# Who copies a transposed pair, and what VectorE does first: slots 5 to 8 of a fused attention and two-layer kernel

## The chip, the core and the metric

The kernel runs on one core of a Trainium2 chip. The core has five engines with a queue each, which they work off in order: TensorE (PE: matmuls, transposes), VectorE (DVE), ScalarE (ACT), GpSimd (POOL) and SyncE (SP); DMAs run beside them. Matmuls write to PSUM, a memory of eight banks from which VectorE and ScalarE read. Engines wait for each other through semaphores. The metric is the device time of one execution in microseconds, median of three runs.

## The reference

For each of 8 batches and 8 heads (sequence S = 576, head width 64) an attention with a decay that comes from a forget gate `f`, and then, over all 4608 tokens, two matrix products with an elementwise function between them:

```
scores = q @ k.T / 8 + (cum[:, None] - cum[None, :])   # cum = cumsum(log(clip(f)))
attn   = softmax(scores with the causal mask);  x = attn @ v
h = x @ w_in            # 512 -> 2048
g = h - tanh(h)
out = g @ w_out         # 2048 -> 512
```

## The kernel before

The attention goes pair by pair of heads: 32 pairs, four to a batch, and the loop at L608 has one slot `p` for each pair, and one more. Slot p holds the scores of pair p in seven tiles (`TILES`, numbers 0 to 6; tile 3 is small and holds the last block of both heads), and pieces of other work put between the tiles by `att_items(p)`. The order is written out by hand: what is emitted first stands first in the queue of its engine.

- `scores` (L306): one to four matmuls of KT and QT into a PSUM bank `ps` (pool `ps_sc`, two banks), then ScalarE's exp into `e` (L335), then from batch 1 on a mask by GpSimd (L345). So the scores of tile t need the bank that the exp of tile t-2 has read.
- `values` (L350): 30 matmuls of `e` and v into `av` for the pair before, and on VectorE the division by the row sums: an add (L364), a reciprocal (L365) and a product into `xn` (L366).
- `turn` (L369): turns `xn` into XR, the input of the products, from slot 5 on by two transposing DMAs on SP's queue.
- `trans` (L254): six transposes on TensorE turn one pair of q or k (rows 6n to 6n+5 of a head lie on one partition) into one PSUM bank, `t32`; from slot 4 on the bank comes from `ps_tr`, which has one. Then it is copied into QT or KT. With `split` false there are two copies, each of both heads: one of the even tokens (partitions 0 to 63 of the bank), one of the odd (64 to 127). With `split` true there are four, one for each head and half, in the order head 0 even, head 0 odd, head 1 even, head 1 odd. The letters in `copies` say which engine makes each: V for VectorE (L277), A for ScalarE (L275). `trans` emits the first two copies and returns the rest, which only the start of the program (L519 on) uses.
- `mlp1(u, ft)` (L398): four matmuls of win and XR into `hps` (pool `ps_m`, three banks), the tanh `th` on ScalarE (L413; pool `tmp`, two buffers), and VectorE's sum of both into `gq` (L417). u counts groups of 512 tokens, ft blocks of 128 columns.
- `mlp2_plain` (L436) for u = 0, `mlp2` (L455) after that: the second product. For u > 0 it goes by a scheme of seven products instead of eight, with sums and differences on VectorE (`sums`) and of the weights (`weights`, L243).

In slots 0 to 3 (`early`) the transposes use other banks. Slots 4 to 6 each transpose q and k of the next pair, by VectorE alone (`"VV"`); in slots 5 and 6 q's stands after tile 0 (`at_q`), k's after tile 3 (`at_k`), and `values` of the pair before after tile 2. The 16 column blocks of `mlp1` for u = 0 are spread over slots 4 to 6: blocks 4 to 10 in slot 5, and blocks 11 to 15 and the first step of `mlp2_plain` in slot 6. Slots 7 and 8 have four transposes each, after tiles 0, 2, 4 and 6 (L569 to L571): q and k of two pairs of batch 2, with `"VA"`. These two slots also have steps of `mlp2_plain` and VectorE's differences of the weights. From batch 3 on q and k are turned by DMA.

Of the kernel before, what the change touches and what calls it, by code (L numbers as in the profile page):

```python
# [11 lines left out]
ALU = mybir.AluOpType  # L12
# [9 lines left out]
def kernel(  # L22
# [10 lines left out]
    nc = tc.nc  # L33
    P = 128

    B, H, S, D = q.shape
# [4 lines left out]
    NPAIR = H // 2  # L41
    NJ = 5
# [38 lines left out]
    qn, kn = ([t[0:S // NT6, :].rearrange("p (h n d) -> p h n d", h=H, n=NT6) for t in raw] for raw in (qraw, kraw))  # L81
    qb, kb = ([t[:, 0:NJ * DM].rearrange("p (n e) -> p n e", n=NJ) for t in raw] for raw in (qraw, kraw))
    vn = [qkp.tile([P, NJ, H, VW], FP16, tag=f"vn{i}", name=f"vn{i}") for i in range(2)]
    QT = [qkp.tile([D + 3, H, S], FP16, tag=f"QT{i}", name=f"QT{i}") for i in range(2)]
    KT = [qkp.tile([D + 3, H, PITCH], FP16, tag=f"KT{i}", name=f"KT{i}") for i in range(2)]
# [89 lines left out]
    def const_rows(i):  # L175
        nc.sync.dma_start(out=QT[i][D:D + 2, :, :], in_=minus16)
        nc.sync.dma_start(out=KT[i][D + 2:D + 3, :, 0:S], in_=ones16[0:H, :])
# [74 lines left out]
    E, XN, GQ, SQ, M2 = {}, {}, {}, {}, {}  # L252

    def trans(b, c, src, dst, early, copies, split=False):  # L254
        pn, g3 = S // NT6, NT6 // 2
        if early:
            t32 = ps_m.tile([P, UW], FP32, tag="m", name="t32")
            t16 = t32.bitcast(FP16)[:, 0:2 * S // 2].rearrange("p (a g n) -> p a g n", a=2, g=g3)
        else:
            t32 = ps_tr.tile([P, UW], FP32, tag="tr", name="t32")  # L260
            t16 = t32.bitcast(FP16)[:, 0:2 * S // 2].rearrange("p (a g n) -> p a g n", a=2, g=g3)
        for a in range(2):
            for g in range(g3):
                nc.tensor.transpose(out=t16[:, a, g, :],  # L264
                                    in_=src[b % 2][:, 2 * c + a, 2 * g:2 * g + 2, :],
                                    identity=id16[0:pn, 0:pn])
        parts = [(a, e) for a in range(2) for e in range(2)] if split else [(slice(0, 2), e) for e in range(2)]

        def copy(a, e, eng):
            if split:  # L270
                a = slice(a, a + 1)
            to = dst[b % 2][0:D, 2 * c:2 * c + 2, e:S:2].rearrange("d a (p g) -> d a p g", g=g3)[:, a]
            of = t16[e * D:(e + 1) * D, :, :, :].rearrange("d a g p -> d a p g")[:, a]
            if eng == "A":
                nc.scalar.activation(out=to, in_=of, func=AF.Copy)  # L275
            else:
                nc.vector.tensor_copy(out=to, in_=of)  # L277

        todo = [lambda a=a, e=e, eng=eng: copy(a, e, eng) for (a, e), eng in zip(parts, copies)]
        for fn in todo[:2]:  # L280
            fn()
        return todo[2:]

    def head_tiles(a):
        return [[(a, 0, 0, 512, 0)],
# [61 lines left out]

    AV = {}

    def values(b, c, heads=(0, 1)):  # L350
        if 0 in heads:
            AV[(b, c)] = ps_av.tile([P, 2, 512], FP32, tag="av", name="av")
        av = AV[(b, c)][:, :, 0:NJ * (D + 1)].rearrange("p a (i d) -> p a i d", i=NJ)
        for a in heads:
            for ib in range(NJ):
                for j in range(ib + 1):
                    nc.tensor.matmul(out=av[:, a, ib, :], lhsT=E.pop((b, c, a, j, ib)),  # L357
                                     rhs=vn[b % 2][:, j, 2 * c + a, 0:D + 1],
                                     start=(j == 0), stop=(j == ib))
        if 1 not in heads:  # L360
            return
        xn = XN[(b, c)] = fin.tile([P, NJ, P], FP16, tag="xn", name="xn")
        rs = fin.tile([P, 2, NJ, 1], FP32, tag="rs", name="rs")
        nc.vector.tensor_scalar_add(out=rs, in0=av[:, :, :, D:D + 1], scalar1=1e-9)  # L364
        nc.vector.reciprocal(out=rs, in_=rs)  # L365
        nc.vector.tensor_tensor(out=xn.rearrange("p i (a d) -> p a i d", a=2), in0=av[:, :, :, 0:D],  # L366
                                in1=rs.to_broadcast([P, 2, NJ, D]), op=ALU.mult)

    def turn(b, c):  # L369
        xn = XN.pop((b, c))  # L370
# [18 lines left out]
    def bank(name):  # L389
        ring = RINGS[turn_of[0]]  # L390
        pool = ring[turn_of[1] % len(ring)]
        turn_of[1] += 1
        return pool.tile([P, UW], FP32, tag=TAGS[pool], name=name)
# [4 lines left out]
    def mlp1(u, ft, part=None):  # L398
        if part != 1:
            HP[(u, ft)] = bank("hps")  # L400
        hps = HP[(u, ft)]
        t0 = u * UW % RING
        parts = [(0, t0, min(UW, RING - t0))]
        if t0 + UW > RING:
            parts.append((RING - t0, 0, t0 + UW - RING))
        for o, t, n in parts:
            for ci in {None: range(NCH), 0: range(NCH - 1), 1: (NCH - 1,)}[part]:
                nc.tensor.matmul(out=hps[:, o:o + n], lhsT=win[:, ci, ft * P:(ft + 1) * P],  # L408
                                 rhs=XR[:, ci, t:t + n], start=(ci == 0), stop=(ci == NCH - 1))
        if part == 0:  # L410
            return
        th = tmp.tile([P, UW], FP32, tag="th", name="th")
        nc.scalar.activation(out=th, in_=hps, func=AF.Tanh, scale=-1.0)  # L413
        half, i, kt = ft // NK, ft % NK // 4, ft % 4
        if half == 0 and kt == 0:
            GQ[(u, i)] = gtp.tile([P, 2, NK // 2, UW], FP16, tag="gq", name="gq")
        nc.vector.tensor_tensor(out=GQ[(u, i)][:, half, kt, :], in0=hps, in1=th, op=ALU.add)  # L417
        if u >= PLAIN:
            if ft in (3, 6, 9, 12):
                sums(u, "S3", ft // 3 - 1)  # L420
# [8 lines left out]
    def sums(u, name, n):  # L429
        i, ks = n // 2, slice(n % 2 * 2, n % 2 * 2 + 2)  # L430
        if name == "S2" and n % 2 == 0:
            SQ[(u, i)] = gtp.tile([P, 2, NK // 2, HU], FP16, tag="sq", name="sq")
        x, y, op = SUMS[name]
        nc.vector.tensor_tensor(out=LHS[name](u, i)[:, ks], in0=LHS[x](u, i)[:, ks], in1=LHS[y](u, i)[:, ks], op=op)
# [112 lines left out]
    def att_items(p):  # L547
        def put(fn, *args):
            items.append((lambda: fn(*args), True))

        items = []
        here = pairs[p] if p < len(pairs) else None
        before = pairs[p - 1] if 0 < p <= len(pairs) else None
        after = pairs[p + 1] if p + 1 < len(pairs) else None
        early = p < NPAIR
        for ti in range(len(TILES)):
            if here and (p > 0 or ti > 1):
                put(scores, *here, ti)
            if p == 1 and ti == 6:
                items.append((lambda: const_rows(1), False))  # L560
                items.append((lambda: load_aug(1), False))
            if early and p > 0 and ti in (0, 6):
                put(unread, 2)
            if p == 1 and ti == 3:
                put(last)
            for load in LOADS.get((p, ti), ()):
                items.append((load, False))
            at_q, at_k = (1, 3) if p == 0 else (0, 1) if early else (0, 2) if p == NPAIR else (0, 3)
            if p in (2 * NPAIR - 1, 2 * NPAIR) and ti % 2 == 0:  # L569
                pair = pairs[2 * NPAIR + 2 * (p - 2 * NPAIR + 1) + ti // 4]  # L570
                put(trans, *pair, *((kn, KT) if ti % 4 else (qn, QT)), False, "VA")  # L571
            if ti == at_q and p < 2 * NPAIR - 1:
                put(trans, *after, qn, QT, early, "VV")
            if p == NPAIR:
                if ti in (3, 4):
                    put(mlp1, 0, ti - 3, 1)
            if ti == at_k and p < 2 * NPAIR - 1:
                put(trans, *after, kn, KT, early, "VV")
            if p == NPAIR:
                if ti == 1:  # L580
                    put(turn, *pairs[p - 2])
                    put(values, *before)
                    put(mlp1, 0, 0, 0)
                elif ti == 2:
                    put(mlp1, 0, 1, 0)
                    put(turn, *before)
            elif early and ti in (2, 3) and before:
                put(values, *before, (ti - 2,))
            elif not early and ti == 2 and before:
                put(values, *before)  # L590
            if p < NPAIR:
                if ti == 1 and p > 1:
                    put(turn, *pairs[p - 2])
            elif p > NPAIR and ti == 3:
                put(turn, *before)
        return items

# [8 lines left out]
    with tc.manual_schedule(engines=FIVE):  # L606
        bulk()
        for p in range(len(pairs) + 1):  # L608
            b, c = divmod(p, NPAIR)
            items = att_items(p)  # L610
# [50 lines left out]
```

## Time and profile before

| what | value |
|---|---|
| median of three runs | 347.95 us (347.94 to 347.99) |
| profiled execution: its time, its span | 347.95 us, 346.2 us |
| busy: PE, PEld, DVE, ACT, POOL | 335.2, 230.6, 261.7, 232.6, 161.3 us |
| chain that ended last, by engine | PE 87%, DVE 6%, ACT 4% |
| granted TensorE clock | 1.00 |

The span goes from the first to the last instruction of the trace; the rest of the time lies around it. Busy time of PE is that of matmuls whose ends are modelled, so that they overlap: a matmul of 512 columns is shown with 0.38 us and the next of its kind starts 0.22 us after it. A row of the timeline gives start, duration, engine, line, operation, and in brackets the idle time before it with what ended it. `L277 DVE COPY KT<-t 64x576 f16` is a copy by VectorE, of 64 partitions and 576 elements on each.

### The profile page before, as it was taken

Reading aid. Unit: us, or ns where it says so; the run is one execution under the profiler, and the core shown is the slowest. Engines: PE = TensorE matmul, PEld = TensorE weight load, DVE = VectorE, ACT = ScalarE, POOL = GpSimd, SP = SyncE. Lnnn points to the kernel's source line nnn. Section 1 sums busy time; section 2 is a strip of 40 time slices with the busy share of each in tenths; the row PEclk is TensorE's granted clock in tenths of the full one; section 3 lists DMA queues with packets and bytes.
Section 4 is the critical chain, followed back from the end, with each engine's and each line's share of the span. In section 5 each row is a group of like instructions: output and inputs, shape, how many; then the busy total and the mean of one; then the engine's idle time right before and its main releaser. Section 6 shows DMA issues by size and latency. Waiting matters only on the chain.

```text
span 346.2 us, 8606 instructions
## 1 busy us (share of the span) xinstructions
PE 335.2 (97%) x3253; PEld 230.6 (67%) x3253; DVE 261.7 (76%) x504; ACT 232.6 (67%) x437; POOL 161.3 (47%) x319
## 2 busy tenths in 40 slices
PE   8988998889999999999999999999999999999995
PEld 7476554555578656865688888755875587487485
DVE  6599787564988788678867886788677766876874
ACT  5687886777897787778767876788548842632640
POOL 8974652676558655765577465742322210000000
PEclk9999999999999999999999999999999999999999
DMA  8999999999999999799979997991131013003003
GB/s 108 147 182 201 193 201 154 107 114 177 132 130 105 177 137 122 94 176 137 117 78 200 130 128 78 186 143 27 49 97 31 17 50 110 0 14 109 0 11 113
DMA packets 144877, 38.80 MB, mean 112 GB/s; under 512 B 128148, under 2 KB 143236, under 8 KB 144836
## 3 DMA queue, kind: packets, MB, share of 16 engines
q0 software_dynamic: 92480, 18.39, 69.7%
q1 hardware_dynamic: 52356, 19.88, 30.5%
q8 instruction: 25, 0.41, 0.5%
q14 instruction: 16, 0.13, 0.1%
HBM read 36.85 MB, written 9.44 MB: 134 GB/s over the span
## 4 chain that ended last, share of the span: by engine, by line
PE 87%; DVE 6%; ACT 4%; issue 1%; DMA 1%; ACTq 0%
PE hps L408 32%; PE ops L466 28%; PE ps L326 12%; PE av L357 8%; PE ops L442 3%; DVE gq L417 2%; ACT e L335 2%; DVE QT L277 2%; PE t L264 1%; DVE KT L277 1%; PE ps L329 1%; DMA TQ<-in_f_dram 1%; PE ps L297 1%; ACT QT L275 1%; ACT th L413 1%
## 5 line engine op out<-in xcount | busy, mean ns | idle before, releaser
L408 PE MATMUL hps<-XR,win 128*128 128x512 f16 (+1 forms) x640 | 140.9, 357 | 0.9 <-ACT XR L378 0.7
L413 ACT ACTIVATE th<-hps 128x512 f32<-128x512 f32 x144 | 86.9, 603 | 55.4 <-PE hps L408 54.6
L335 ACT ACTIVATE e<-ps 128x512 f16<-128x512 f32 x192 | 110.5, 598 | 14.1 <-PE ps L326 6.0
L417 DVE TENSOR_TENSOR gq<-hps,th 128x512 f16<-128x512 f32 x144 | 98.4, 688 | 26.0 <-ACT th L413 24.6
L345 POOL TENSOR_SCALAR_AFFINE_SELECT e<-e 128x128 f16<-128x128 f16 x168 | 60.4, 361 | 78.0 <-ACT e L335 76.1
L408 PEld LDWEIGHTS <-win 128*128 128x128 f16 x640 | 57.7, 97 | 48.4 <-issue 0.5
L326 PE MATMUL ps<-QT,KT 67*128 67x64 f16 (+5 forms) x384 | 77.9, 276 | 3.1 <-ACT e L335 1.7
L466 PEld LDWEIGHTS <-gq 128*128 128x128 f16 x640 | 60.4, 97 | 11.1
L466 PE MATMUL ops<-wout,gq 128*128 128x256 f16 x512 | 63.2, 272 | 0.0
L326 PEld LDWEIGHTS <-KT 67*128 67x128 f16 (+1 forms) x384 | 36.7, 98 | 25.5 <-DVE KT L277 1.6
L357 PEld LDWEIGHTS <-e 128*128 128x128 f16 x896 | 32.2, 97 | 3.9
L357 PE MATMUL av<-vn,e 128*128 128x65 f16 x896 | 33.6, 193 | 0.0
L119 POOL DMA_DIRECT2D vn<-in_v_dram x32 | 28.0, 878 | 8.7 <-DMA win<-in_moe_w_in_dram 4.1
L466 PE MATMUL ops<-W,sq 128*128 128x256 f16 x256 | 31.2, 272 | 0.0
L366 DVE TENSOR_TENSOR xn<-av,rs 128x640 f16<-128x640 f32 x32 | 26.4, 825 | 1.1
L466 PEld LDWEIGHTS <-sq 128*128 128x128 f16 x256 | 24.2, 98 | 3.4
L96 POOL DMA_DIRECT2D kn<-in_k_dram x25 | 21.2, 848 | 1.5 <-issue 1.3
L345 POOL TENSOR_SCALAR_AFFINE_SELECT el<-el 128x128 f16<-128x128 f16 x28 | 9.4, 334 | 26.9 <-ACT el L335 26.2
L96 POOL DMA_DIRECT2D qn<-in_q_dram x25 | 21.2, 848 | 1.3 <-issue 0.8
L364 DVE TENSOR_SCALAR rs<-av 128x10 f32<-128x10 f32 x32 | 5.2, 162 | 19.0 <-PE av L357 17.9
L277 DVE COPY QT<-t 64x576 f16<-64x576 f16 x18 | 14.5, 803 | 6.2 <-PE t L264 6.1
L277 DVE COPY KT<-t 64x576 f16<-64x576 f16 (+1 forms) x22 | 16.3, 739 | 3.8 <-PE t L264 3.6
(82 smaller groups left out, 307.5 us busy)
## 6 DMA issues: line engine op xcount, KB each, us to landing
out_dram<-ost SPq DMA_DIRECT2D x34, 256.0 KB
vn<-in_v_dram POOLq DMA_DIRECT2D x24, 128.0 KB, 5.6
qn<-in_q_dram POOLq DMA_DIRECT2D x20, 128.0 KB, 4.3
kn<-in_k_dram POOLq DMA_DIRECT2D x20, 128.0 KB, 4.6
win<-in_moe_w_in_dram POOLq DMA_DIRECT2D x2, 1024.0 KB, 14.8
wout<-in_moe_w_out_dram POOLq DMA_DIRECT2D x2, 1024.0 KB, 14.1
XR<-xn SPq DMA_TRANSPOSE x56
vn<-in_v_dram POOLq DMA_DIRECT2D x12, 64.0 KB, 5.2
```

The source lines that it names most:

```text
L96: nc.gpsimd.dma_start(out=dst[b % 2][0:pn, n, :].rearrange("p (h d) -> p h d", h=H), in_=src[b, :, n * P:n * P + pn, :].rearrange("h p d - ...
L119: nc.gpsimd.dma_start(out=vn[b % 2][:, n, h0:h1, 0:D], in_=v[b, h0:h1, n * P:(n + 1) * P, :].rearrange("h p d -> p h d"))
L277: nc.vector.tensor_copy(out=to, in_=of)
L326: nc.tensor.matmul(out=ps[:, col:col + n], lhsT=KT[b % 2][0:rows, h, j * P:(j + 1) * P], rhs=QT[b % 2][0:rows, h, i0:i0 + n], start=not ow ...
L335: nc.scalar.activation(out=e[:, lo:hi], in_=ps[:, lo:hi], func=AF.Exp, scale=qscale)
L345: nc.gpsimd.affine_select(out=view, in_=view, compare_op=ALU.is_ge, fill=0.0, base=0, pattern=pat, channel_multiplier=-1)
L357: nc.tensor.matmul(out=av[:, a, ib, :], lhsT=E.pop((b, c, a, j, ib)), rhs=vn[b % 2][:, j, 2 * c + a, 0:D + 1], start=(j == 0), stop=(j == ib))
L366: nc.vector.tensor_tensor(out=xn.rearrange("p i (a d) -> p a i d", a=2), in0=av[:, :, :, 0:D], in1=rs.to_broadcast([P, 2, NJ, D]), op=ALU. ...
L408: nc.tensor.matmul(out=hps[:, o:o + n], lhsT=win[:, ci, ft * P:(ft + 1) * P], rhs=XR[:, ci, t:t + n], start=(ci == 0), stop=(ci == NCH - 1))
L413: nc.scalar.activation(out=th, in_=hps, func=AF.Tanh, scale=-1.0)
L417: nc.vector.tensor_tensor(out=GQ[(u, i)][:, half, kt, :], in0=hps, in1=th, op=ALU.add)
L466: nc.tensor.matmul(out=ps[:, m, :], lhsT=LHS[lhs](u, kt // 4)[:, kt % 4, m * P:(m + 1) * P], rhs=rhs[:, kt, :], start=(fresh and (apart or ...
```

## The change

It has two parts. In slots 7 and 8 the transposes are copied with `"VVAA"` and `split` true, and `trans` emits all four copies at once: VectorE copies head 0 (even and odd tokens), ScalarE head 1. There `values`, which stood behind the transposes of k after tile 2, is put ahead of them.

In slots 5 and 6 `values` no longer emits the division but leaves it in a list, `HELD`. While that list is not empty, the sums of `mlp1` (L417) are appended to it too. After tile 3, behind the transposes and copies of k and ahead of `turn`, the list is emitted in its order.

```
-        for fn in todo[:2]:
+        now = 4 if copies == "VVAA" else 2
+        for fn in todo[:now]:
             fn()
-        return todo[2:]
+        return todo[now:]
...
+    HELD = []
+
+    def release():
+        while HELD:
+            HELD.pop(0)()
+
-    def values(b, c, heads=(0, 1)):
+    def values(b, c, heads=(0, 1), hold=False):
...
-        nc.vector.tensor_scalar_add(out=rs, in0=av[:, :, :, D:D + 1], scalar1=1e-9)
-        nc.vector.reciprocal(out=rs, in_=rs)
-        nc.vector.tensor_tensor(out=xn.rearrange("p i (a d) -> p a i d", a=2), in0=av[:, :, :, 0:D],
-                                in1=rs.to_broadcast([P, 2, NJ, D]), op=ALU.mult)
+
+        def divide():
+            nc.vector.tensor_scalar_add(out=rs, in0=av[:, :, :, D:D + 1], scalar1=1e-9)
+            nc.vector.reciprocal(out=rs, in_=rs)
+            nc.vector.tensor_tensor(out=xn.rearrange("p i (a d) -> p a i d", a=2), in0=av[:, :, :, 0:D],
+                                    in1=rs.to_broadcast([P, 2, NJ, D]), op=ALU.mult)
+
+        HELD.append(divide)
+        if not hold:
+            release()
...
-        nc.vector.tensor_tensor(out=GQ[(u, i)][:, half, kt, :], in0=hps, in1=th, op=ALU.add)
+
+        def add_up():
+            nc.vector.tensor_tensor(out=GQ[(u, i)][:, half, kt, :], in0=hps, in1=th, op=ALU.add)
+
+        if HELD:
+            HELD.append(add_up)
+        else:
+            add_up()
...
             if p in (2 * NPAIR - 1, 2 * NPAIR) and ti % 2 == 0:
+                if ti == 2:
+                    put(values, *before)
                 pair = pairs[2 * NPAIR + 2 * (p - 2 * NPAIR + 1) + ti // 4]
-                put(trans, *pair, *((kn, KT) if ti % 4 else (qn, QT)), False, "VA")
+                put(trans, *pair, *((kn, KT) if ti % 4 else (qn, QT)), False, "VVAA", True)
...
-            elif not early and ti == 2 and before:
+            elif p in (NPAIR + 1, NPAIR + 2) and ti == 2:
+                put(values, *before, (0, 1), True)
+            elif not early and ti == 2 and before and p not in (2 * NPAIR - 1, 2 * NPAIR):
                 put(values, *before)
...
             elif p > NPAIR and ti == 3:
+                items.append((release, False))
                 put(turn, *before)
```

## The prediction

> **What bounds the kernel now.** I read the busy time by stretches first, to see where TensorE is not full. Columns: busy us and (instructions) of each engine, granted clock, DMA share, GB/s.
>
> ```profile
> 43.00:56.50 13.50, 12.16 (x104) 6.41 (x102) 12.36 (x21) 10.11 (x20) 6.35 (x16) 1.00 1.52 193
> 56.50:80.00 23.50, 21.03 (x196) 11.87 (x197) 12.99 (x22) 16.73 (x28) 13.71 (x27) 1.00 1.42 126
> 80.00:120.00 40.00, 40.00 (x394) 26.77 (x393) 32.53 (x63) 31.52 (x61) 27.17 (x50) 1.00 1.42 140
> ```
>
> From 80 us on TensorE is busy without a gap (also in the stretches to 280 and 320), at a granted clock of 1.00. A delay or a gain that exists at 80 us therefore reaches the end one for one: no later idle time takes a delay in. Slots 5 to 8, which the change touches, lie in the first two stretches (slot 5 about 38 to 47 us, slot 6 to 56.6, slot 7 to 66.6, slot 8 to 77.1). Next, TensorE's waits:
>
> ```profile
> PE ps L326 <- ACT e L335: 1.7, 5, 0.5
> PE t L264 <- ACT QT L275: 1.7, 4, 0.4
> PE ps L326 <- DVE KT L277: 1.1, 1, 1.1
> PE t L264 <- ACT KT L275: 0.3, 1, 0.3
> PE hps L408 <- DVE gq L417: 0.2, 1, 0.2
> ```
>
> The wait on KT is the first score of slot 7. The waits of `t` are transposes that need their only PSUM bank (`ps_tr`, one buffer) back. Then the timeline of VectorE, ScalarE and TensorE around them (start, us, engine, line):
>
> ```profile
> 43.80 0.82 DVE L366 TENSOR_TENSOR xn<-av,rs 128x640 f16<-128x640 f32 x1
> 44.54 0.68 DVE L417 TENSOR_TENSOR gq<-hps,th 128x512 f16<-128x512 f32 x1
> 45.14 1.60 DVE L277 COPY KT<-t 64x576 f16<-64x576 f16 x2
> 46.77 2.11 DVE L417 TENSOR_TENSOR gq<-hps,th 128x512 f16<-128x512 f32 x3
> ```
> ```profile
> 45.32 0.60 ACT L413 ACTIVATE th<-hps 128x512 f32<-128x512 f32 x1 [0.31 <-PE hps L408]
> 47.56 0.60 ACT L413 ACTIVATE th<-hps 128x512 f32<-128x512 f32 x1 [0.67 <-DVE gq L417]
> ```
> ```profile
> 45.51 1.03 PE L408 MATMUL hps<-XR,win 128*128 128x512 f16 x4
> 47.52 1.02 PE L408 MATMUL hps<-XR,win 128*128 128x512 f16 x4 [0.20 <-DVE gq L417]
> 56.57 0.39 PE L326 MATMUL ps<-QT,KT 67*128 67x512 f16 x1 [1.10 <-DVE KT L277]
> 59.82 0.41 PE L264 MATMUL t<-id,kn 96*128 96x96 f16 x6 [0.43 <-ACT QT L275]
> ```
> ```profile
> 58.12 0.80 DVE L277 COPY QT<-t 64x576 f16<-64x576 f16 x1 [0.88 <-PE t L264]
> ```
> ```profile
> 58.95 0.81 ACT L275 ACTIVATE QT<-t 64x576 f16<-64x576 f16 x1 [1.29 <-DVE QT L277]
> ```
>
> Two things matter. At 47.52 and 47.56 both TensorE and ScalarE wait for one `gq` sum: `hps` has three banks and `th` two buffers, so the sum of column block n frees the bank of block n+3 and the buffer of block n+2. And the transpose at 57.66 ends at 58.08, VectorE copies 58.12 to 58.92, and only then, 0.03 us later, ScalarE copies to 59.77: the two copies of one transpose run one after the other, in all eight transposes of slots 7 and 8, 0.80 + 0.03 + 0.81 = 1.65 us. Last, the prices by form:
>
> ```profile
> L277 DVE COPY QT<-t 64x576 f16<-64x576 f16 x18 | 14.5, 803 | 6.2 <-PE t L264 6.1
> L275 ACT ACTIVATE QT<-t 64x576 f16<-64x576 f16 x4 | 3.2, 812 | 3.3 <-DVE QT L277 3.3
> L275 ACT ACTIVATE QT<-t 64x288 f16<-64x288 f16 x4 | 2.0, 489 | 1.2 <-PE t L264 1.1
> L277 DVE COPY KT<-t 64x288 f16<-64x288 f16 x4 | 1.9, 476 | 0.1
> ```
>
> **Slot 5: the held sum.** In the order of the changed program VectorE does: sums 5 and 6, k's two copies, the division (L364 to L366), sum 7, sums 8 and on. Only sum 7 is held back. The kn transposes end at 43.51, so the copies run 43.55 to 45.16 (1.60), the division to 46.46 (43.36 to 44.63 before, 1.27 with its gaps), sum 7 to 47.05 (44.54 + 0.68 = 45.22 before), sum 8 to 47.66. Sum 7 is 1.83 later. Queued behind it: TensorE's block 10 needs its bank and goes from 45.51 to 47.11; ScalarE's tanh of block 9 needs its buffer and goes from 45.32 to 47.15. Behind that tanh stand the exps of tiles 4 and 5 on ScalarE (cadence 0.48): they end 48.23 and 48.72. TensorE's tile 6 waits for the bank of tile 4 (48.28, was 46.45) and slot 6's first score for that of tile 5 (48.77, was 46.94); block 11 starts 0.22 later at 48.99 instead of 47.52. Loss 1.47. The 0.20 wait for sum 8 and the 0.11 wait before slot 6's first score go, both hidden inside this.
>
> **Slot 6: what the order gains.** From 48.99 TensorE repeats its cadence (7.57 us from block 11 to tile 6): tile 6 at 56.56. K's copies now run 54.56 to 56.17, ahead of the division, so the first score of slot 7 (KT) no longer waits for them; late next is the bank of tile 5, whose exp ends at 57.00 (block 15's tanh at 55.42, then exps at 0.48). It starts at 57.05: 0.49 us after tile 6, against 55.09 to 56.57, 1.48, before. Gain 0.99. Sum 14 is held too, but no tanh follows it before slot 9, and `ops` in slot 7 needs it only at 60.6, when it has been done since 58.1. The division ends 3.1 us later (57.5 against 54.4), and with it the two transposing DMAs to XR on SP; the first matmul that reads XR for block u=1 is past 82 us, and SP has nothing to issue between 57 and 62 but these.
>
> **Slots 7 and 8: the split copies.** Each transpose now has four 64x288 copies: VectorE two for head 0, 2 x 0.476 + 0.01 = 0.97; ScalarE two for head 1, 2 x 0.49 + 0.01 = 1.00. In the built program ScalarE's first copy still waits for the count that VectorE's second copy brings, so a transpose takes 0.97 + 0.03 + 1.00 = 2.00 us where it took 1.65: 0.35 more, eight times. If the wait were not there it would take about 1.0; this is the lower end of the unknown cost, and the first rival. I take 2.00, because the eight rows of before show the wait and the changed program keeps it.
> The row first: ScalarE's eight copies start 0.03 us behind VectorE's, never beside them. The Trainium skill, "PSUM — Partial Sum Buffer", section "PSUM bank collisions raise a hardware error", says that two engines must not touch one bank in the same 32-partition quadrant at once, reads with reads included, and calls guarding by bank the simple version; both heads of a transpose lie in the same partitions of one bank. By that rule the copies stay in turn, and the sum is the one here; its finer form, by quadrant, would have let the old halves (partitions 0 to 63 and 64 to 127) run together, and the trace does not show that.
>
> Now the path, with the latencies of before (TensorE's end to a copy 0.04, a copy's end to TensorE 0.05, to the next exp 0.02). k's transposes of tile 2 also stand behind `values` and one `ops` step now, at no cost in TensorE's work, but VectorE's division stands ahead of their copies. Transposes a to d are slot 7's, e to h slot 8's. Starting from 57.05:
> a at 58.13 (57.66 before), copies done 60.63; b at 61.46 (59.82), no wait, its old 0.59 wait is covered by values and ops (1.77 us). av starts 59.69, the division runs 60.80 to 62.07, b's copies to 62.96 and 64.00, so c, wanted at 63.73, starts 64.05 (63.85). c's copies end 66.52: d, wanted 65.64, starts 66.57 (66.00). The exp of tile 5 stands behind c's copies on ScalarE and ends 67.14: slot 8's first score 67.19 (66.62). d's copies end 69.03: e, wanted 68.27, starts 69.08 (68.14). f at 72.41 (70.29 with its 0.59 wait, which values and ops cover). Division to 73.0, f's copies to 74.94: g at 74.98 (74.32). g's copies, behind slot 8's last `ost`, end 77.44: h at 77.49 (76.47). Slot 9's first score waits for the exp of tile 5: 78.11 (77.09). h's copies end 79.95 on ScalarE and hold back slot 9's first exp to 80.57, which frees the bank of tile 2: 80.62 (79.25).
> From slot 7's first score to there: 23.57 against 22.68, loss 0.89. The waits that the move removes (two of 0.59) are less than what the longer copies add at c, d, e, g, h and behind.
>
> **Sum.** +1.47 − 0.99 + 0.89 = +1.37 us at 80 us, carried to the end. The profiled execution took 347.95 (span 346.2 and 1.7 outside it), which is the median of the runs too: 349.3. ScalarE's extra (8 x 0.19) and VectorE's (8 x 0.17) are inside this; the weights' differences (L245) move behind copies, but are read from slot 10 on.
>
> **The rivals.**
> Side by side: if the copies of the two heads did overlap, each transpose would be free 1.0 us after its end. Redoing the same path, the waits at b, c, d, f and g go, h and e keep 0.2 and 0.4, slot 9's first score is at 75.26: 1.83 earlier than before, 346.1. It decides as soon as ScalarE's copy starts over 0.5 us before VectorE's second ends. Against it: the eight rows and the kept wait. A page speaks for it: the Trainium skill, "Perfetto Trace Analysis", section "Optimizing Scalar/DVE Operations", says that breaking up instructions may let work finish sooner where an engine makes others idle; here no reader of the bank is served by half of it.
> The held sum costs nothing: if block 10's bank or the tanh's buffer came from elsewhere, slot 5 stays as it is, and −0.99 + 0.89 leaves −0.1: 347.85, no change. It decides if sum 7 ended before 45.5. Against it: 47.52 and 47.56 show exactly this dependence for the next sum.
> No recovery in slot 6: if VectorE's lag pushed k's copies past 57 again, as in the 1.10 wait of before, the 0.99 is lost: 350.3. Against it: they end 0.9 before they are needed.
>
> **How the numbers follow.** 0.2% is 0.7 us, about what a measurement of this kernel tells from no change. Forecast 0.71 (its own range 348.7 to 349.9, a third of a microsecond of error in each of the three parts), no recovery 0.08, held sum free 0.08, side by side 0.13. The range 347.6 to 350.4 takes in all but the last. Slower takes the forecast, but for a few parts in a hundred near the bound, and no recovery: 0.77; same 0.11; faster 0.12.
>
> **What would show it.** In the new trace: one wait of TensorE's `hps` on VectorE's sum of about 1.5 us near 47 us; no wait on KT at slot 7; ScalarE's 64x288 copies 0.03 us behind VectorE's second; `t` waiting near 66, 69 and 77 us by 0.8 to 0.9; the stretch after 82 us as before, only later. Wrong if ScalarE's copies begin together with VectorE's, or if the first score of slot 6 stands before 48 us.

## The result, and the profile after

The changed kernel takes 349.69 us (median of six runs, 349.67 to 351.36) against 347.95 (347.93 to 347.99): a ratio of 1.0058, 95% interval 1.004 to 1.0076 (of the means; the medians alone give 1.0050). It is 1.74 us slower; forecast were 1.35 more, 349.3. Single executions of several of these kernels take 1.5 to 3 us longer than the others (351.36 here), which leaves the median where it is but raises the mean.

Its line numbers differ from those of before: L421 is `hps` (was L408), L426 the tanh (L413), L432 the sum (L417), L375 the division's product (L366), L336 the exp (L335), L327 the scores (L326), L462 `ops` of u = 0 (L442). L264, L275 and L277 are as they were. First the busy time by stretches, cut at 57.05, where slot 7 begins, and at 82.00, in slot 9 behind the last wait that the slots cause (columns: busy us and instructions of PE, PEld, DVE, ACT, POOL; granted clock; DMA share; GB/s):

```profile
43.00:57.05 14.05, 12.25 (x104) 6.58 (x103) 11.71 (x20) 9.42 (x20) 5.79 (x14) 1.00 1.51 192
57.05:82.00 24.95, 21.61 (x198) 12.03 (x198) 14.90 (x31) 18.53 (x37) 16.32 (x28) 1.00 1.21 122
82.00:120.00 38.00, 38.00 (x385) 25.95 (x384) 31.18 (x61) 29.95 (x58) 25.52 (x48) 1.00 1.42 130
```

TensorE is again full from 82 us on, at a clock of 1.00. Set instruction against instruction, TensorE is 1.48 us later in slot 6, 1.65 at the first `hps` of slot 9, and still 1.65 at 225 us: what the slots lose reaches the end. (0.07 more comes near 230 us. It shows in the trace of the part in slots 7 and 8 alone too, not in that of slots 5 and 6; its cause is open.) TensorE's waits:

```profile
PE ps L327 <- ACT e L336: 2.1, 7, 0.5
PE t L264 <- ACT QT L275: 1.6, 2, 0.8
PE hps L421 <- DVE gq L432: 1.4, 1, 1.4
PE t L264 <- ACT KT L275: 1.1, 3, 0.7
```

The wait of a score for KT (1.1 before) is gone. In its place stand one wait of `hps` for a sum, 1.4 us (0.2 before), and waits of `t` that are as many but longer: 2.7 us over five times against 2.0 over five. The timelines of slot 5 (VectorE; ScalarE; TensorE, with the first score of slot 7 last):

```profile
43.55 1.61 DVE L277 COPY KT<-t 64x576 f16<-64x576 f16 x2
45.63 0.82 DVE L375 TENSOR_TENSOR xn<-av,rs 128x640 f16<-128x640 f32 x1
46.38 2.10 DVE L432 TENSOR_TENSOR gq<-hps,th 128x512 f16<-128x512 f32 x3
```
```profile
47.15 0.60 ACT L426 ACTIVATE th<-hps 128x512 f32<-128x512 f32 x1 [2.14 <-DVE gq L432]
```
```profile
47.11 1.02 PE L421 MATMUL hps<-XR,win 128*128 128x512 f16 x4 [1.43 <-DVE gq L432]
48.99 1.03 PE L421 MATMUL hps<-XR,win 128*128 128x512 f16 x4
57.06 0.38 PE L327 MATMUL ps<-QT,KT 67*128 67x512 f16 x1
```

Copies, division, then the sums: the first of the three sums from 46.38 on is that of block 7, which the list had held, and both TensorE's block 10 and ScalarE's tanh of block 9 start right behind it. And slot 7's and 8's copies (VectorE; ScalarE; TensorE's transposes):

```profile
64.55 0.97 DVE L277 COPY QT<-t 64x288 f16<-64x288 f16 x2 [1.01 <-PE t L264]
```
```profile
65.61 0.98 ACT L275 ACTIVATE QT<-t 64x288 f16<-64x288 f16 x2 [0.78 <-DVE QT L277]
```
```profile
64.09 0.41 PE L264 MATMUL t<-id,qn 96*128 96x96 f16 x6 [0.20 <-ACT KT L275]
66.65 0.42 PE L264 MATMUL t<-id,kn 96*128 96x96 f16 x6 [0.79 <-ACT QT L275]
69.20 0.41 PE L264 MATMUL t<-id,qn 96*128 96x96 f16 x6 [0.69 <-ACT KT L275]
```

VectorE's two copies of the transpose at 64.09 end at 65.52, ScalarE's start at 65.61 and end at 66.60, and the next transpose starts at 66.65. The two engines copy in turn, as before, only longer: 0.97 + 0.09 + 0.98 = 2.04 us against 1.65.

### The profile page after: what moved, and what is told of

The parts are those of the page before. It is cut to its first block, busy times and chain, and to the rows that moved or that the text cites. A ratio compares the mean times of both kernels' runs of the same rounds, so it can differ in the third digit from the quotient of the medians.

```text
span 348.0 us, 8637 instructions
## 1 busy us (share of the span) xinstructions
PE 335.4 (96%) x3253; PEld 230.5 (66%) x3253; DVE 263.0 (76%) x512; ACT 233.5 (67%) x445; POOL 163.0 (47%) x319
## 4 chain that ended last, share of the span: by engine, by line
PE 91%; DVE 3%; ACT 3%; issue 1%; DMA 1%; ACTq 0%
PE hps L421 35%; PE ops L486 28%; PE ps L327 13%; PE av L364 8%; PE ops L462 2%; PE t L264 2%; ACT e L336 1%; DVE KT L277 1%; PE ps L330 1%; DMA TQ<-in_f_dram 1%; PE ps L298 1%; ACT KT L275 1%; PE ps L296 0%; DVE TQ L159 0%; PE x L390 0%
## 5 line engine op out<-in xcount | busy, mean ns | idle before, releaser
L421 PE MATMUL hps<-XR,win 128*128 128x512 f16 (+1 forms) x640 | 140.9, 357 | 2.1 <-DVE gq L432 1.4
L426 ACT ACTIVATE th<-hps 128x512 f32<-128x512 f32 x144 | 86.9, 603 | 56.9 <-PE hps L421 54.8
L432 DVE TENSOR_TENSOR gq<-hps,th 128x512 f16<-128x512 f32 x144 | 98.4, 688 | 26.8 <-ACT th L426 25.3
L336 ACT ACTIVATE e<-ps 128x512 f16<-128x512 f32 x192 | 110.4, 598 | 12.2 <-PE ps L330 4.8
L346 POOL TENSOR_SCALAR_AFFINE_SELECT e<-e 128x128 f16<-128x128 f16 x168 | 62.1, 371 | 78.5 <-ACT e L336 76.6
L421 PEld LDWEIGHTS <-win 128*128 128x128 f16 x640 | 57.8, 97 | 49.8 <-issue 1.8
L327 PE MATMUL ps<-QT,KT 67*128 67x64 f16 (+5 forms) x384 | 77.9, 276 | 2.5 <-ACT e L336 2.1
L327 PEld LDWEIGHTS <-KT 67*128 67x128 f16 (+1 forms) x384 | 36.8, 98 | 24.6 <-issue 2.1
L375 DVE TENSOR_TENSOR xn<-av,rs 128x640 f16<-128x640 f32 x32 | 26.4, 825 | 1.1
L277 DVE COPY QT<-t 64x576 f16<-64x576 f16 (+1 forms) x22 | 15.1, 685 | 6.9 <-PE t L264 6.7
L277 DVE COPY KT<-t 64x576 f16<-64x576 f16 (+1 forms) x26 | 16.9, 650 | 3.2 <-PE t L264 2.8
```

Of the source, the lines that this page charges most:

```text
L327: nc.tensor.matmul(out=ps[:, col:col + n], lhsT=KT[b % 2][0:rows, h, j * P:(j + 1) * P], rhs=QT[b % 2][0:rows, h, i0:i0 + n], start=not ow ...
L336: nc.scalar.activation(out=e[:, lo:hi], in_=ps[:, lo:hi], func=AF.Exp, scale=qscale)
L346: nc.gpsimd.affine_select(out=view, in_=view, compare_op=ALU.is_ge, fill=0.0, base=0, pattern=pat, channel_multiplier=-1)
```

## The experiments

The theory: the change is two parts that add. In slots 5 and 6 the held sum costs and the early copies gain; in slots 7 and 8 the split copies cost, because both heads lie in one PSUM bank, and the earlier `values` gains. The rivals: the held sum is harmless; the division ahead of k's copies is what costs; the copies are kept in turn by their destination and not by the bank. Times of before in these runs: 347.95 and 347.97. The diffs are against the changed kernel where they say "changed", else against the kernel before.

**The part in slots 5 and 6 alone** (changed kernel, slots 7 and 8 put back)

```
-                if ti == 2:
-                    put(values, *before)
...
-                put(trans, *pair, *((kn, KT) if ti % 4 else (qn, QT)), False, "VVAA", True)
+                put(trans, *pair, *((kn, KT) if ti % 4 else (qn, QT)), False, "VA")
...
-            elif not early and ti == 2 and before and p not in (2 * NPAIR - 1, 2 * NPAIR):
+            elif not early and ti == 2 and before:
```

> The part in slots 5 and 6 alone (division and late sums behind k's copies); slots 7 and 8 as before. If the parts add up as in the prediction: slot 5 loses 1.47 (block 10 and the tanh of block 9 wait for the held sum 7), slot 6 gains 0.99, so slot 7's first score stands at 57.05 instead of 56.57 and all after it is 0.48 later: 348.4 us. Rival, the held sum costs nothing: block 10 stays near 45.5 and the time is 347.0. Rival, slot 6 gives nothing back: 349.4.

Measured: 348.48 us, ratio 1.0029 (1.0016 to 1.0042). TensorE in slot 5 and at slot 7's first scores:

```profile
47.09 1.02 PE L421 MATMUL hps<-XR,win 128*128 128x512 f16 x4 [1.43 <-DVE gq L432]
56.54 0.87 PE L327 MATMUL ps<-QT,KT 67*128 67x320 f16 x3
57.25 1.03 PE L462 MATMUL ops<-wout,gq 128*128 128x512 f16 x4
```

Block 10 waits as in the full change, and the first score of slot 7 follows the last of slot 6 in one row: the wait on KT is gone. The `ops` behind it stood at 56.80 before. Loss and recovery are both there, 0.53 net; both rivals on this part fall.

**The part in slots 7 and 8 alone** (changed kernel, nothing held)

```
-            elif p in (NPAIR + 1, NPAIR + 2) and ti == 2:
-                put(values, *before, (0, 1), True)
```

> The part in slots 7 and 8 alone (split copies, values ahead of k's transposes); slots 5 and 6 as before. By the prediction's path this part costs 0.89; with the gap of 0.09 instead of 0.03 us between VectorE's second copy and ScalarE's first, which the changed kernel's trace shows, 1.17: 349.1 us. Rival, the parts depend on each other (VectorE's lag from slot 6 makes slot 7 slow): nearer to before, under 348.6.

Measured: 349.24 us, ratio 1.0056 (1.0034 to 1.0079): +1.29. With +0.53 of the other part that makes +1.82, and the whole change is +1.74: the parts add, but for 0.08.

**Only the division held, the sums where they were** (the first experiment, and:)

```
-        if HELD:
-            HELD.append(add_up)
-        else:
-            add_up()
+        add_up()
```

> As the part in slots 5 and 6 alone, but only the division is held back, the sums are emitted where they were. Sum 7 then ends near 44.5, so block 10 and the tanh of block 9 do not wait; but sum 8 stands behind copies and division and ends near 48.0 instead of 47.47, so block 11 is some 0.5 late; slot 7's first score near 56.2 instead of 56.57: 347.6 us. If the held sum is not what makes slot 5 slow, the time is that of the part with the sums held, 348.4.

Measured: 347.32 us, ratio 0.9982 (0.9973 to 0.999). ScalarE's tanh of block 9 and TensorE's first score of slot 7:

```profile
45.28 0.60 ACT L426 ACTIVATE th<-hps 128x512 f32<-128x512 f32 x1 [0.27 <-PE hps L421]
```
```profile
55.74 0.39 PE L327 MATMUL ps<-QT,KT 67*128 67x512 f16 x1 [0.26 <-DVE KT L277]
```

The tanh waits for its own matmuls again, and the part gains 0.63 instead of losing 0.53. The difference, 1.16 us, is what holding the sums costs: those of blocks 7 and 8 in slot 5 and that of block 14 in slot 6. It gained 0.3 more than expected: sum 8 came ahead of the division too, since block 8 is emitted before the list is (so the changed kernel holds its sum as well), and block 11 did not wait; in its place block 12 waited 0.24 for sum 9.

**Only `values` moved in slots 7 and 8, copies as before**

```
             if p in (2 * NPAIR - 1, 2 * NPAIR) and ti % 2 == 0:
+                if ti == 2:
+                    put(values, *before)
...
-            elif not early and ti == 2 and before:
+            elif not early and ti == 2 and before and p not in (2 * NPAIR - 1, 2 * NPAIR):
```

> Only values put ahead of k's transposes in slots 7 and 8; copies unsplit as before (VectorE even tokens, ScalarE odd), slots 5 and 6 as before. If the longer copies are what costs in slots 7 and 8, the move itself is a gain: values and one ops step cover the bank's release at the second and the sixth transpose, two waits of 0.59 go and none comes: 346.8 us. Rival, the division ahead of k's copies is what costs: the third and the seventh transpose wait, and the time is 348 or more.

Measured: 346.81 us, ratio 0.9967 (0.9955 to 0.9979). Transposes a to d of slot 7:

```profile
57.66 0.42 PE L264 MATMUL t<-id,qn 96*128 96x96 f16 x6
60.99 0.42 PE L264 MATMUL t<-id,kn 96*128 96x96 f16 x6
63.26 0.42 PE L264 MATMUL t<-id,qn 96*128 96x96 f16 x6
65.41 0.41 PE L264 MATMUL t<-id,kn 96*128 96x96 f16 x6 [0.42 <-ACT QT L275]
```

The second waits no more, and the third doesn't wait although the division now stands ahead of k's copies. The move is a gain of 1.14, twice the wait of 0.59; the rival that blames the division falls.

**Only the copies split, `values` where it was** (and `trans` emits all four copies, as in the change)

```
-                put(trans, *pair, *((kn, KT) if ti % 4 else (qn, QT)), False, "VA")
+                put(trans, *pair, *((kn, KT) if ti % 4 else (qn, QT)), False, "VVAA", True)
```

> Only the split copies (VectorE head 0, ScalarE head 1, one bank) in slots 7 and 8; values where they were, slots 5 and 6 as before. If the copies stay in turn, a transpose's bank is free 2.06 us after its end instead of 1.65: the four waits of 0.59 and the one of 0.44 grow by 0.4 to 0.46 each, and slot 9's third tile waits 0.4: +2.4 to +2.7, 350.4 to 350.7 us. If the split itself were harmless and the division ahead of the copies the cost: 348 or less.

Measured: 350.47 us, ratio 1.0067 (1.0052 to 1.0082): +2.50. Transposes b, d and e:

```profile
60.23 0.42 PE L264 MATMUL t<-id,kn 96*128 96x96 f16 x6 [0.83 <-ACT QT L275]
66.82 0.42 PE L264 MATMUL t<-id,kn 96*128 96x96 f16 x6 [0.83 <-ACT QT L275]
69.37 0.41 PE L264 MATMUL t<-id,qn 96*128 96x96 f16 x6 [0.69 <-ACT KT L275]
```

Each wait of 0.43 (as the profile counts it, from the modelled end) has become 0.83. The split alone is the loss, and the move takes 1.23 of it back (350.47 to 349.24).

**The two heads in two banks** (the part in slots 7 and 8 alone, and the edit below; transposes and copies of head a then use `t16[a]`)

```
+        elif copies == "VVAA":
+            t16 = [pool.tile([P, UW], FP32, tag=tag, name="t32").bitcast(FP16)[:, 0:S // 2]
+                   .rearrange("p (a g n) -> p a g n", a=1, g=g3) for pool, tag in ((ps_tr, "tr"), (ps_m, "m"))]
         else:
```

> As the part in slots 7 and 8 alone (349.24), but head 1 of each transpose goes to a bank of its own (from the three of ps_m), so VectorE and ScalarE read different banks. If the shared bank is what keeps the copies in turn, ScalarE's first copy starts 0.04 us after the transposes end, beside VectorE's; a bank is free after 1.05 us and the waits of the transposes go: by the path 345.5 us. If it is the destination (one QT or KT tile for both) or something else, ScalarE still starts behind VectorE and the time stays near 349.2 or above.

Measured: 345.28 us, ratio 0.9926 (0.9905 to 0.9946). VectorE's and ScalarE's copies of the first transpose of slot 7 (L283 and L281 here), and their mean by form (four of ScalarE's twelve belong to the start of the program):

```profile
57.99 0.97 DVE L283 COPY QT<-t 64x288 f16<-64x288 f16 x2 [0.76 <-PE t L267]
```
```profile
58.12 0.99 ACT L281 ACTIVATE QT<-t 64x288 f16<-64x288 f16 x2 [0.46 <-PE t L267]
```
```profile
L281 ACT ACTIVATE QT<-t 64x288 f16<-64x288 f16 x12 | 5.9, 488 | 2.0 <-PE t L267 1.9
L283 DVE COPY QT<-t 64x288 f16<-64x288 f16 x8 | 3.8, 478 | 2.5 <-PE t L267 2.5
```

ScalarE's copies start when head 1's transposes end (58.08), beside VectorE's, in spite of the common destination QT, and none of the single copies is slower for it (478 and 488 ns; 476 and 489 before). In all eight transposes ScalarE starts before VectorE's second copy ends, by 0.08 to 1.05 us. The part in slots 7 and 8 goes from a loss of 1.29 to a gain of 2.69. Both hold the 1.14 that the move gains by itself; without it, the split costs 2.43 in one bank and gains 1.55 in two. The common bank was the reason that the copies went in turn; as a bank is also one tile of the program here, the run does not tell the bank from the tile. Head 1's bank comes from a pool of three, and so seldom has to be waited for; an estimate from the ends of ScalarE's copies in this trace is that one second bank alone would have held up two of the eight transposes, by 0.15 and 0.03 us. The rule cited in the prediction (the Trainium skill, "PSUM — Partial Sum Buffer", "PSUM bank collisions raise a hardware error") agrees with this, and so does a sentence of that page's section "Specifications (TRN2)", that the two engines read PSUM in parallel at full rate as long as they don't meet in a bank. No run shows what the chip would do without the wait: it is set when the program is built, and was not taken away.

**The two gaining halves together** (changed kernel, only slot 6 held, copies unsplit)

```
-            elif p in (NPAIR + 1, NPAIR + 2) and ti == 2:
+            elif p == NPAIR + 2 and ti == 2:
...
-                put(trans, *pair, *((kn, KT) if ti % 4 else (qn, QT)), False, "VVAA", True)
+                put(trans, *pair, *((kn, KT) if ti % 4 else (qn, QT)), False, "VA")
```

> The gaining halves together: division and late sum held in slot 6 alone (slot 5 as before), values ahead of k's transposes in slots 7 and 8, copies unsplit. If slot 6's gain of 0.99 and the move's 1.14 (measured alone) add up: 345.8 us. If slot 6's gain was only the recovery of time lost in slot 5, it is that of the move alone, 346.8.

Measured: 345.78 us, ratio 0.9932 (0.9915 to 0.9948): −2.19; less the 1.14 of the move, slot 6 gives 1.05. Slot 6's gain is its own, and not a recovery of what slot 5 lost.

**A version without these waits** (changed kernel, only slot 6 held; the transposes after tiles 4 and 6 copied by VectorE alone, the one after tile 6 in a bank of `ps_m`)

```
-            t32 = ps_tr.tile([P, UW], FP32, tag="tr", name="t32")
+            t32 = (ps_m if other else ps_tr).tile([P, UW], FP32, tag="m" if other else "tr", name="t32")
...
-                put(trans, *pair, *((kn, KT) if ti % 4 else (qn, QT)), False, "VVAA", True)
+                put(trans, *pair, *((kn, KT) if ti % 4 else (qn, QT)), False, "VV" if ti > 3 else "VA", False, ti == 6)
```

> A version that takes the waits away: division and late sum held in slot 6 alone, values moved, and the transposes after tiles 4 and 6 copied by VectorE alone, the one after tile 6 in a bank of ps_m. ScalarE's exp of tile 5 then stands behind no copy, and no transpose needs a bank in use. All waits of slots 6 to 8 (4.8 us) but about 0.3 would go: 343.5 us if VectorE, with 5 us more to do in slots 7 and 8, keeps up; up to 345 if it becomes late with the division or slot 9's sums.

Measured: 343.62 us, ratio 0.9879 (0.9858 to 0.99): the fastest of all, 4.35 below before. Its busy time in slots 7 and 8 (columns as above; all rows of this trace stand 1.9 us later from the first slots on, so the cut is later):

```profile
58.50:80.00 21.50, 21.50 (x232) 12.92 (x230) 17.08 (x29) 13.91 (x26) 17.14 (x31) 1.00 1.54 134
```

TensorE is busy without a gap there, and VectorE, with 17.08 of 21.50 us, keeps up.

## Why the prediction came out as it did

**Where delays go.** That everything at 80 us is carried to the end held: the delay at the first `hps` of slot 9 is 1.65, the median's 1.74.

**Slot 5, the held sum.** Right step by step: block 10 at 47.11 (47.11 worked out), block 11 at 48.99 (48.99), loss 1.47. One sentence was not: "Only sum 7 is held back" leaves out sum 8, which goes into the list too. It did not change the numbers: held, or emitted behind the list as the working took it, sum 8 stands right behind sum 7. The pair of experiments with and without the sums held shows the cause, not only the place.

**Slot 6, the early copies.** Right: the first score of slot 7 is released by the bank of tile 5, not by KT, and stands at 57.06 (57.05 worked out). The gain, 0.99 in the working, is 1.05 by the run of both gaining halves less that of the move.

**Slots 7 and 8, the split copies.** The mechanism was right (copies in turn, waits at c, d, e, g and h and at slot 9's third tile, none at b and f), and one term of the sum was mis-sized: the step "0.97 + 0.03 + 1.00" took the gap between the engines from before. It is 0.09. The transposes stood at 58.13, 61.47, 64.09, 66.65, 69.20, 72.53, 75.17 and 77.72 against 58.13, 61.46, 64.05, 66.57, 69.08, 72.41, 74.98 and 77.49 worked out, the miss growing where a wait decides. Slot 9's third tile is at 80.91 (80.62): 0.29 of the 0.39 us missed. Another 0.07 is the unexplained step near 230 us; the last 0.03 are open.

**The rivals.** "Side by side" did not happen, for the reason given; the two-bank run gives its size: 345.28 without the part in slots 5 and 6, where the rival's path would have had 345.6 (its 346.1 less the 0.48 of that part). "The held sum costs nothing" and "no recovery" are excluded by the first experiment (348.48, against 347.0 and 349.4).

## What to carry to other kernels

Before work is split between two engines, ask whether both halves lie in one PSUM bank: in one bank this program has them go in turn, and the split only adds the fixed time of more instructions and a later start of the second engine (2.04 us against 1.65 here), while in two banks the same split gained. When an instruction is moved to the back of a queue, look for what its operands' buffers hold up: here one postponed sum stopped two engines, since its inputs were the oldest of three banks and of two buffers. And cut a change into its parts: this one held two gains (1.05 and 1.14) beside two losses that outweighed them.

## What the runs showed of the hardware that was not expected

ScalarE's start behind VectorE's copy took 0.09 us in all eight transposes of the changed kernel (for one, VectorE's end at 65.52 and ScalarE's start at 65.61), but 0.03 in all eight of before. In the built programs the copy of before waits for one semaphore; that of the changed kernel waits for TensorE, and a separate instruction ahead of it waits for VectorE. In the trace that separate instruction starts 0.03 us after VectorE's end in all eight (65.55 in the one above), as the copy itself did before, and the copy follows 0.06 behind it. The tanh at 47.15 has the same two waits and started 0.09 after the sum that it waited for. That the separate wait is what costs the 0.06 us is argued from these rows; no run tested it by itself.
